# Weight sums of a two-stage mixture kernel: differences on VectorE, sums as adding transfers

## The chip, the cores and the metric

The kernel runs on one core of a Trainium2 chip. The metric is the device time of one execution in microseconds (us). In the profile PE is TensorE (PEld its weight loads), DVE is VectorE, ACT is ScalarE, POOL is GpSimd and SP is SyncE, which issues most transfers.

## The reference

Attention (a band of keys and block summaries), then a mixture in which each token goes to one expert, then a second mixture in which all 1536 tokens go through all 8 experts. The change touches the weights of the second mixture alone:

```python
def _moe2_ref(x, w_gate, w1, w2):
    N, D = x.shape                       # 1536, 512
    E = w_gate.shape[1]                  # 8
    logits = x @ w_gate
    ...                                  # 8 turns that normalise P over experts and tokens
    for e in range(E):
        h = np.maximum(x @ w1[e], 0.0)   # w1[e]: 512 x 1024
        ye = h @ w2[e]                   # w2[e]: 1024 x 512
        out += P[:, e:e + 1] * ye
```

## The kernel before

The second mixture starts at about 320 us of the span and lasts to its end. Both products of an expert are computed by a scheme of Strassen's kind: each matrix is cut into four quarters, and seven products of quarters, or of sums of quarters, replace eight. An fp32 factor is split into an fp16 part and an fp16 rest (`hi` and `lo`), and three products of these stand for one.

The program of this part is written out by hand in *ticks*. In a tick PE does one step of the first product (`first`, L1251: six matmuls into `fx` or `fa`) and, in every other tick, one step of the second product (`second`, L1337: twelve matmuls into `gx` or `ga`). One expert's first products take 84 ticks: 3 chunks of 512 tokens, 4 blocks `fc` of hidden units, 7 ticks each. Everything else is put at a tick by `at(tick, f)`, and each engine runs its instructions in the order in which the ticks issue them. In each block of seven ticks the engines do this beside PE:

- ACT copies products out of PSUM (`take`, L1258), ACT or DVE adds the others (`add`, L1261).
- For the block before, DVE forms the four sums of the hidden quarters in place in `c` (L1297 to L1300, fp32, 128x256 each), ACT casts them to fp16 (L1303, `hh`), and DVE forms the rest (L1306, `hl`). ACT reaches L1303 in its own order, and the `take`s of the next block stand behind it.
- Results of `second` go to `acc` by DVE (L1368) or by ACT into `y` (L1376), which POOL issues as an adding transfer (L1370, L1378).

The weights of the coming expert are prepared in the same ticks. A `Piece` is one of the four blocks of w1 or w2 of an expert; a raw buffer `raw` holds six quarters of 128x256 fp32, and three buffers take turns. A piece goes through: `load` (SP, ticks ahead), for most pieces `measure` (ACT, its square sum), `measured` and `rate` (a power of two as scale), `sums(0)`, `sums(1)`, `sums(2)` and `sum4` (L707 and L711: the four sums of quarters, on POOL), `raw_hi` and `raw_lo` (the three plain quarters: ACT L715 and DVE L720, 128x768), `sum_hi` and `sum_lo` (the four sums: the same lines, 128x1024). In one step three quarters are overwritten in place, so that `sum4` may run only when `raw_lo` has read the plain ones. `begin` is the tick of `raw_hi`; `raw_lo`, `sum4` follow one and two ticks later, `sum_hi` and `sum_lo` six and seven ticks later. For the last piece of w2 (`last`) these ticks hang on a step of `second`. `weigh(e)` (L1204) scales the expert's gate column `pws` at the start of its second product.

The eight pieces of expert 0 are prepared during the first mixture (`plain`), and there DVE forms the sums. In the transposition of the tokens (`tokens`, `part4`, L1077) the rests of `T3` and `T4` are formed by POOL for five of six pairs.

Of the kernel before, what the change touches and what calls it, by code (L numbers as in the profile page):

```python
# [18 lines left out]
ALU = mybir.AluOpType  # L19
# [30 lines left out]
K2 = KC // 2  # L50
# [58 lines left out]
def body(ctx: ExitStack, tc: tile.TileContext, q, k, v, wg1, w1a, w2a, wg2, w1b, w2b, cst, out):  # L109
    nc = tc.nc  # L110
# [41 lines left out]
    with ExitStack() as st:  # L152
# [29 lines left out]
        for i in range(3):  # L182
            t = a1.tile([P, NW, 2, D], F32, name=f"vt{i}")
            eng = nc.gpsimd if i else nc.vector
# [42 lines left out]
        sums = {}  # L227
# [58 lines left out]
        def queries(u):  # L286
# [26 lines left out]
            out=wg2_sb.rearrange("p (k e) -> p k e", k=KC), in_=wg2.rearrange("(k p) e -> p k e", p=P)  # L313
# [248 lines left out]
        for t in range(S // P, NTB):  # L562
# [3 lines left out]
            out=nb3,  # L566
            in0=cnt.unsqueeze(2).to_broadcast([P, E, 6]),
            in1=c_(C_BEG, 6 * E).rearrange("p (e j) -> p e j", e=E),
            op=ALU.is_gt,
# [5 lines left out]
            out=bs3,  # L575
            in0=nb.unsqueeze(1).to_broadcast([P, E, E]),
            in1=c_(C_LT, E * E).rearrange("p (e f) -> p e f", e=E),
            op=ALU.mult,
# [5 lines left out]
            out=bend, in0=nb[0:1], scalar=float(CAP), in1=base[0:1], op0=ALU.mult, op1=ALU.add  # L584
# [3 lines left out]
            out=eb3,  # L588
            in0=bend.unsqueeze(1).to_broadcast([1, NBLK, E]),
            in1=c_(C_BLK, NBLK * E)[0:1].rearrange("p (n e) -> p n e", e=E),  # L590
            op=ALU.is_le,
# [8 lines left out]
        with tc.issue_after(eblk.ins):  # L600
# [7 lines left out]
            out=at_tile,  # L608
# [54 lines left out]
    class Piece:  # L663
# [35 lines left out]
            nc.tensor.matmul(pf, ones_b, sqb[self.x][:, self.i : self.i + 1], start=True, stop=True)  # L699
            pow2(pf, wsc[self.x][:, self.i : self.i + 1], gsc[self.x][:, self.i : self.i + 1])  # L700

        def sums(self, only=None, eng=nc.gpsimd):
            o = own[id(self.raw)]; assert o is self, (self.e, self.second, self.j, o.e, o.second, o.j)
            r = [self.raw[:, i] for i in range(6)]
            todo = ((4, 3, 0, -1), (5, 4, 1, -1), (3, 3, 1, -1)) if self.second else ((5, 0, 3, -1), (4, 5, 1, -1), (3, 3, 1, 1))
            for to, x, y, sign in todo if only is None else todo[only : only + 1]:
                eng.tensor_tensor(out=r[to], in0=r[x], in1=r[y], op=ALU.add if sign > 0 else ALU.subtract)  # L707

        def sum4(self, eng=nc.gpsimd):
            o = own[id(self.raw)]; assert o is self, (self.e, self.second, self.j, o.e, o.second, o.j)  # L710
            eng.tensor_tensor(out=self.raw[:, 2], in0=self.raw[:, 2], in1=self.raw[:, 5 if self.second else 4], op=ALU.add)  # L711

        def hi(self, w, s):
            o = own[id(self.raw)]; assert o is self, (self.e, self.second, self.j, o.e, o.second, o.j)
# [135 lines left out]
    if True:  # L850
# [112 lines left out]
        def plain(i, p):  # L963
            idle = lambda: None
            raw = raws[i % 3]
            junk = raw[:, 4:6].rearrange("p a f -> p (a f)").bitcast(BF16)
            return [lambda: p.load(raw), idle, idle, lambda: p.measure(junk), p.measured, p.rate, lambda: (p.raw_hi(), p.sums(eng=nc.vector)), lambda: (p.raw_lo(), p.sum4(eng=nc.vector)),
                    idle, p.sum_hi, p.sum_lo]

        more = weave(  # L970
# [72 lines left out]
    def tokens(j):  # L1043
# [30 lines left out]
        def parts(to, x, eng):  # L1074
            hi, lo = (y[:, to[0] : to[-1] + 1, :, cols].rearrange("p a k t -> p (a k) t") for y in (sh, sl))
            nc.scalar.copy(hi, x)  # L1076
            eng.tensor_tensor(out=lo, in0=x, in1=hi, op=ALU.subtract)  # L1077
# [25 lines left out]
            parts((B22,), quarters()[3], nc.vector)  # L1103

        def part4():
            parts((T3, T4), t4[:, 2 * K2 :], nc.gpsimd if j else nc.vector)

        def part5():
            b12 = quarters()[2]
# [211 lines left out]
    def second(e, k, s, i):  # L1321
# [18 lines left out]
        if (k, s) == (CHUNKS - 1, 1) and e + 1 in last:  # L1340
            if i == 4:
                p4 = last[e + 1]
                for d, f in zip((0, 1, 2, 5, 6), (p4.raw_hi, p4.raw_lo, p4.sum4, p4.sum_hi, p4.sum_lo)):
                    at(clock[0] + 1 + d, f)
        ts = [2 * k + s + h * HTB for h in range(2)]
        lo, hi, both = slice(0, Q), slice(Q, DM), slice(0, DM)
# [93 lines left out]
    for want, p, begin, measure in sorted(jobs, key=lambda x: x[0]):  # L1440
        i = min(range(len(raws)), key=lambda i: (max(free[i], want), -free[i]))
        load = max(free[i], want)
        s = TICKS * CHUNKS * p.e
        at(load, lambda p=p, i=i: p.load(raws[i]))
        if measure:
            junk = raws[i][:, 4:6].rearrange("p a f -> p (a f)").bitcast(BF16)
            at(load + 5, lambda p=p, junk=junk: p.measure(junk))
            at(load + 7, p.measured)
            at(load + 11, p.rate)
            assert load + 11 <= s - 3, (p.e, p.second, p.j, load - s)  # L1450
            end = load + 5
        if begin is not None:
            for i_ in range(3):
                at(load + 7 + i_, lambda p=p, i_=i_: p.sums(i_))
            if p.second and p.j == F2 - 1:
                last[p.e] = p
                end = s + 41
                assert load < s + 18, (p.e, p.second, p.j, load - s)
            else:
                begin = max(begin, load + 13)  # L1460
                at(begin, p.raw_hi)
                at(begin + 1, p.raw_lo)
                at(begin + 2, p.sum4)
                end = begin + 7
                at(end - 1, p.sum_hi)
                at(end, p.sum_lo)
                assert end <= s + (39 if p.second else 7 * p.j + 1), (p.e, p.second, p.j, end - s)
                assert begin <= s + (37 if p.second else 7 * p.j - 1), (p.e, p.second, p.j, begin - s)
        free[i] = end + 1
# [53 lines left out]
```

## Time and profile before

| | us |
|---|---|
| median of 3 runs | 1281.98 |
| lowest and highest run | 1281.65, 1283.81 |
| the profiled execution: time | 1283.4 |
| the profiled execution: span, first to last instruction | 1281.5 |

| engine | busy us | share of the span |
|---|---|---|
| PE | 1194.4 | 93% |
| DVE | 1024.4 | 80% |
| ACT | 848.9 | 66% |
| POOL | 368.1 | 29% |

The profiled execution lies 1.4 us above the median, and 1.9 us of it lie outside the span. Shares of the whole span mix three parts of the program; what a change in the second mixture is worth is to be read from the stretch from 320 us on, and from who waits for whom there.

### The profile page before, as it was taken

To read this page: it belongs to the slowest core of one execution; us is meant where nothing else is said; L and a number is where in the kernel's file an instruction comes from. 1 tells how busy PE (TensorE), PEld (TensorE's weight loads), DVE (VectorE), ACT (ScalarE), POOL (GpSimd) and SP (SyncE) were. 2 spreads that over 40 slices of the span, in tenths; PEclk is the share of its full clock that TensorE was granted. 3 is DMA by queue.
4 is the path that set the end of the run, shared out by engine and by line. 5 is a ranking of instruction groups with operands and counts; after the bars stand their busy time and mean duration, and the time that the engine had idled before them with its cause. 6 is when DMAs were issued, how large, how long until landed. Compare 5 with 4: busy or idle time off the path is not lost.

```text
span 1281.5 us, 27664 instructions
## 1 busy us (share of the span) xinstructions
PE 1194.4 (93%) x10551; PEld 1050.3 (82%) x10551; DVE 1024.4 (80%) x1801; ACT 848.9 (66%) x1605; POOL 368.1 (29%) x434
## 2 busy tenths in 40 slices
PE   6898999998799899889999998999899899989998
PEld 5776878887678788778888887888788788878887
DVE  6785678874788888797988798788979888886765
ACT  5676578764777667666767776677667667766541
POOL 4351212112113443332332333242413333322000
PEclk8899999999999999999999999999999999999999
DMA  9954888755325343445543563544445435534301
GB/s 203 204 98 147 275 258 258 243 189 179 122 96 175 110 119 93 113 111 137 133 108 91 127 171 91 131 110 108 124 132 147 114 79 138 143 93 106 84 34 50
DMA packets 178461, 174.38 MB, mean 136 GB/s; under 512 B 32960, under 2 KB 150336, under 8 KB 177936
## 3 DMA queue, kind: packets, MB, share of 16 engines
q1 hardware_dynamic: 163888, 143.75, 38.7%
q0 software_dynamic: 14432, 28.78, 11.5%
q8 instruction: 85, 1.39, 0.5%
q14 instruction: 56, 0.46, 0.1%
HBM read 136.10 MB, written 15.53 MB: 118 GB/s over the span
## 4 chain that ended last, share of the span: by engine, by line
PE 55%; DVE 20%; ACT 9%; DMA 8%; issue 7%; SPq 1%; POOL 0%; DVEq 0%; ACTq 0%; POOLq 0%
PE gx L1337 13%; PE fx L1251 13%; PE fa L1251 10%; PE ga L1337 10%; DMA raw<-in_moe_w 4%; PE ph L814 3%; PE py L833 2%; DVE c L1297 2%; DVE w2l L720 2%; ACT raw L690 2%; DVE c L1298 2%; DVE c L1261 2%; DVE w1l L720 2%; DVE c L1299 1%; DVE hl L1294 1%
## 5 line engine op out<-in xcount | busy, mean ns | idle before, releaser
L1251 PEld LDWEIGHTS <-w1h 128*128 128x128 f16 x2688 | 259.5, 98 | 75.6 <-issue 42.8
L1337 PEld LDWEIGHTS <-hh 128*128 128x128 f16 x2688 | 264.0, 98 | 32.5 <-issue 1.2
L1251 PE MATMUL fx<-xh,w1h 128*128 128x256 f16 x736 | 201.1, 273 | 31.5 <-ACT c L1258 29.7
L1337 PE MATMUL gx<-w2l,hh 128*128 128x256 f16 x768 | 210.4, 274 | 3.0 <-DVE w2l L720 3.0
L1337 PE MATMUL gx<-w2h,hh 128*128 128x256 f16 x768 | 210.5, 274 | 1.0 <-DVE acc L1368 1.0
L1337 PE MATMUL gx<-w2h,hl 128*128 128x256 f16 x768 | 210.3, 274 | 0.0
L1251 PE MATMUL fx<-xl,w1h 128*128 128x256 f16 x736 | 201.3, 274 | 1.0 <-POOL xl L1077 1.0
L1251 PE MATMUL fx<-xh,w1l 128*128 128x256 f16 x736 | 201.4, 274 | 0.0
L707 POOL TENSOR_TENSOR raw<-raw 128x256 f32<-128x256 f32 x168 | 162.3, 975 | 66.0 <-ACT raw L690 41.5
L1303 ACT CAST hh<-c 128x1024 f16<-128x1024 f32 x96 | 100.2, 1043 | 116.0 <-DVE c L1300 115.9
L1258 ACT ACTIVATE c<-fx,kap 128x256 f32<-128x256 f32 x288 | 132.6, 471 | 58.3 <-PE fx L1251 57.7
L1306 DVE TENSOR_TENSOR hl<-c,hh 128x1024 f16<-128x1024 f32 x96 | 123.7, 1288 | 42.8 <-ACT hh L1303 42.7
L1337 PE MATMUL ga<-w2h,hh 128*128 128x256 f16 x576 | 157.2, 273 | 0.0
L1337 PE MATMUL ga<-w2l,hh 128*128 128x256 f16 x576 | 157.1, 273 | 0.0
L1337 PE MATMUL ga<-w2h,hl 128*128 128x256 f16 x576 | 157.0, 273 | 0.0
L1251 PE MATMUL fa<-xh,w1h 128*128 128x256 f16 x552 | 150.8, 273 | 0.9 <-ACT xh L1076 0.9
L1251 PE MATMUL fa<-xl,w1h 128*128 128x256 f16 x552 | 150.8, 273 | 0.5 <-DVE xl L1077 0.5
L1251 PE MATMUL fa<-xh,w1l 128*128 128x256 f16 x552 | 150.7, 273 | 0.0
L1337 PEld LDWEIGHTS <-hl 128*128 128x128 f16 x1344 | 132.0, 98 | 19.8 <-issue 4.1
L1251 PEld LDWEIGHTS <-w1l 128*128 128x128 f16 x1344 | 132.0, 98 | 17.9 <-issue 1.6
L1294 DVE SCALAR_TENSOR_TENSOR hl<-c,hh 128x768 f16<-128x768 f32 x96 | 94.8, 988 | 19.7 <-ACT hh L1291 19.4
L1376 ACT ACTIVATE y<-gx,pws 128x256 f32<-128x256 f32 x144 | 68.1, 473 | 62.3 <-PE gx L1337 34.4
(262 smaller groups left out, 2625.1 us busy)
## 6 DMA issues: line engine op xcount, KB each, us to landing
raw<-in_moe_w SPq DMA_DIRECT2D x64, 512.0 KB, 4.6
raw<-in_moe_w SPq DMA_DIRECT2D x228, 128.0 KB, 2.9
xh<-xohd SPq DMA_DIRECT2D x147, 128.0 KB, 3.0
xl<-xold SPq DMA_DIRECT2D x147, 128.0 KB, 3.2
acc<-y POOLq DMA_DIRECT2D x72, 256.0 KB, 4.3
raw<-in_moe_w SPq DMA_DIRECT2D x38, 256.0 KB, 3.3
vt<-in_v SPq DMA_DIRECT2D x16, 240.0 KB, 9.3
raw<-yd SPq DMA_DIRECT2D x12, 260.0 KB, 3.0
```

The costliest lines, as they stand in the source:

```text
L690: nc.scalar.activation(junk, raw, AF.Square, accum_out=ssq[self.x][:, self.i : self.i + 1])
L707: eng.tensor_tensor(out=r[to], in0=r[x], in1=r[y], op=ALU.add if sign > 0 else ALU.subtract)
L720: nc.vector.scalar_tensor_tensor(out=lo[:, w], in0=self.raw[:, s], scalar=wsc[self.x][:, self.i : self.i + 1], in1=hi[:, w], op0=ALU.mult, ...
L814: nc.tensor.matmul(ph, a, c[:, kc], start=kc == 0 and m == 0, stop=kc == KC - 1 and m == 2)
L833: nc.tensor.matmul(pys[s], a, c, start=fc == 0 and m == 0, stop=fc == FC - 1 and m == 2)
L1251: nc.tensor.matmul(p, l[:, a, kc * P : (kc + 1) * P], r[:, j, kc], start=new and kc == 0 and m == 0, stop=kc == K2 - 1 and m == 2, skip_gr ...
L1258: nc.scalar.activation(c[:, q], p, f, scale=k_)
L1294: nc.vector.scalar_tensor_tensor(out=h[1][:, :3], in0=raw, scalar=0.0, in1=h[0][:, :3], op0=ALU.max, op1=ALU.subtract)
L1303: nc.scalar.copy(h[0][:, 3:], c)
L1306: nc.vector.tensor_tensor(out=h[1][:, 3:], in0=c, in1=h[0][:, 3:], op=ALU.subtract)
L1337: nc.tensor.matmul(p, l, r, start=new and f == 0 and m == 0, stop=f == F2 - 1 and m == 2, skip_group_check=True)
L1376: nc.scalar.activation(gs[h][:, d], p, AF.Copy, scale=w)
```

## The change

For the experts 1 to 7 the sums of quarters leave POOL's arithmetic. A difference is now a `tensor_tensor` on DVE; a sum whose target already holds one of its terms is now an adding transfer that POOL issues (`add`, from SBUF to SBUF, 128x256 fp32). By the instruction lists POOL loses 168 + 56 tensor operations of 128x256; DVE gains 140 at `sums` and 7 at `sum4` (the `last` pieces); POOL issues 77 adding transfers, 28 of them at `sums(2)` of w1 pieces and 49 at `sum4`. `part4` goes wholly to DVE. Three tick rules change: `sum_hi` and `sum_lo` come eight and nine ticks after `begin` instead of six and seven; a piece that is not measured again may begin 8 ticks after its load instead of 13; for `last` pieces `sum_hi` and `sum_lo` come one tick earlier.

```diff
--- before.py
+++ after.py
@@ -699,16 +699,26 @@
             nc.tensor.matmul(pf, ones_b, sqb[self.x][:, self.i : self.i + 1], start=True, stop=True)
             pow2(pf, wsc[self.x][:, self.i : self.i + 1], gsc[self.x][:, self.i : self.i + 1])
 
-        def sums(self, only=None, eng=nc.gpsimd):
+        def add(self, to, of):
+            nc.gpsimd.dma_start(out=self.raw[:, to], in_=self.raw[:, of], accum_op=ALU.add)
+
+        def sums(self, only=None, fast=False):
             o = own[id(self.raw)]; assert o is self, (self.e, self.second, self.j, o.e, o.second, o.j)
             r = [self.raw[:, i] for i in range(6)]
             todo = ((4, 3, 0, -1), (5, 4, 1, -1), (3, 3, 1, -1)) if self.second else ((5, 0, 3, -1), (4, 5, 1, -1), (3, 3, 1, 1))
             for to, x, y, sign in todo if only is None else todo[only : only + 1]:
-                eng.tensor_tensor(out=r[to], in0=r[x], in1=r[y], op=ALU.add if sign > 0 else ALU.subtract)
-
-        def sum4(self, eng=nc.gpsimd):
+                if sign > 0 and not fast:
+                    self.add(to, y)
+                else:
+                    nc.vector.tensor_tensor(out=r[to], in0=r[x], in1=r[y], op=ALU.add if sign > 0 else ALU.subtract)
+
+        def sum4(self, fast=False):
             o = own[id(self.raw)]; assert o is self, (self.e, self.second, self.j, o.e, o.second, o.j)
-            eng.tensor_tensor(out=self.raw[:, 2], in0=self.raw[:, 2], in1=self.raw[:, 5 if self.second else 4], op=ALU.add)
+            of = 5 if self.second else 4
+            if fast:
+                nc.vector.tensor_tensor(out=self.raw[:, 2], in0=self.raw[:, 2], in1=self.raw[:, of], op=ALU.add)
+            else:
+                self.add(2, of)
 
         def hi(self, w, s):
             o = own[id(self.raw)]; assert o is self, (self.e, self.second, self.j, o.e, o.second, o.j)
@@ -964,7 +974,7 @@
             idle = lambda: None
             raw = raws[i % 3]
             junk = raw[:, 4:6].rearrange("p a f -> p (a f)").bitcast(BF16)
-            return [lambda: p.load(raw), idle, idle, lambda: p.measure(junk), p.measured, p.rate, lambda: (p.raw_hi(), p.sums(eng=nc.vector)), lambda: (p.raw_lo(), p.sum4(eng=nc.vector)),
+            return [lambda: p.load(raw), idle, idle, lambda: p.measure(junk), p.measured, p.rate, lambda: (p.raw_hi(), p.sums(fast=True)), lambda: (p.raw_lo(), p.sum4(fast=True)),
                     idle, p.sum_hi, p.sum_lo]
 
         more = weave(
@@ -1103,7 +1113,7 @@
             parts((B22,), quarters()[3], nc.vector)
 
         def part4():
-            parts((T3, T4), t4[:, 2 * K2 :], nc.gpsimd if j else nc.vector)
+            parts((T3, T4), t4[:, 2 * K2 :], nc.vector)
 
         def part5():
             b12 = quarters()[2]
@@ -1340,7 +1350,7 @@
         if (k, s) == (CHUNKS - 1, 1) and e + 1 in last:
             if i == 4:
                 p4 = last[e + 1]
-                for d, f in zip((0, 1, 2, 5, 6), (p4.raw_hi, p4.raw_lo, p4.sum4, p4.sum_hi, p4.sum_lo)):
+                for d, f in zip((0, 1, 2, 4, 5), (p4.raw_hi, p4.raw_lo, lambda: p4.sum4(True), p4.sum_hi, p4.sum_lo)):
                     at(clock[0] + 1 + d, f)
         ts = [2 * k + s + h * HTB for h in range(2)]
         lo, hi, both = slice(0, Q), slice(Q, DM), slice(0, DM)
@@ -1457,11 +1467,11 @@
                 end = s + 41
                 assert load < s + 18, (p.e, p.second, p.j, load - s)
             else:
-                begin = max(begin, load + 13)
+                begin = max(begin, load + (13 if measure else 8))
                 at(begin, p.raw_hi)
                 at(begin + 1, p.raw_lo)
                 at(begin + 2, p.sum4)
-                end = begin + 7
+                end = begin + 9
                 at(end - 1, p.sum_hi)
                 at(end, p.sum_lo)
                 assert end <= s + (39 if p.second else 7 * p.j + 1), (p.e, p.second, p.j, end - s)
```

On DVE, between expert 2 and expert 3: `w1l1` and `w1l0` are rests of weights of expert 3's w1 pieces 1 and 0, the rows of `c` alone are the hidden sums (L1297 to L1300). Before:

```order
L720 SCALAR_TENSOR_TENSOR w1l0_1677<-raw1_1711,wsc1_1699,w1h0_1676 128x1024
L1294 SCALAR_TENSOR_TENSOR hl_10066<-c_9862,hh_10065 128x768
L1261 SCALAR_TENSOR_TENSOR c_9979<-fx_9978,kap0_1700,c_9979 128x256
L1368 SCALAR_TENSOR_TENSOR acc_5495<-ga_9944,pws_5498,acc_5495 128x512
L720 SCALAR_TENSOR_TENSOR w1l1_1679<-raw2_1712,wsc1_1699,w1h1_1678 128x768
L694 CAST sqb1_1695<-ssq1_1693 128x1
L1297 SCALAR_TENSOR_TENSOR c_9862<-c_9862 128x256
L1298 TENSOR_TENSOR c_9862<-c_9862 128x256
L1299 TENSOR_TENSOR c_9862<-c_9862 128x256
L1300 TENSOR_TENSOR c_9862<-c_9862 128x256
```

And now (the same lines of the program stand ten lines lower, so L1307 is the old L1297, L1316 the old L1306 that makes the rest `hl` of the sums, L730 the old L720):

```order
L730 SCALAR_TENSOR_TENSOR w1l1_1679<-raw2_1712,wsc1_1699,w1h1_1678 128x768
L694 CAST sqb1_1695<-ssq1_1693 128x1
L713 TENSOR_TENSOR raw1_1711<-raw1_1711 128x256
L1307 SCALAR_TENSOR_TENSOR c_9861<-c_9861 128x256
L1308 TENSOR_TENSOR c_9861<-c_9861 128x256
L1309 TENSOR_TENSOR c_9861<-c_9861 128x256
L1310 TENSOR_TENSOR c_9861<-c_9861 128x256
L730 SCALAR_TENSOR_TENSOR w1l0_1677<-raw0_1710,wsc1_1699,w1h0_1676 128x1024
L713 TENSOR_TENSOR raw1_1711<-raw1_1711 128x256
L627 TENSOR_SCALAR gsc1_1697<-pz_5486 128x1
L630 TENSOR_SCALAR wsc1_1699<-gsc1_1697 128x1
L1316 TENSOR_TENSOR hl_10065<-c_9861,hh_10064 128x1024
```

One difference of the next piece (L713) stands ahead of the four hidden sums and one behind them, and the long rest of piece 0 (128x1024), which stood four rows ahead of that of `w1l1`, comes behind the four sums and ahead of `hl`.

On ACT at the same place (L1258, L1303, L1376 and L715 of before are L1268, L1313, L1386 and L725 now). Before:

```order
L715 ACTIVATE w1h0_1676<-raw1_1711,wsc1_1699 128x1024
L690 ACTIVATE raw0_1710,ssq1_1693<-raw0_1710 128x1024
L1291 ACTIVATE hh_10065<-c_9862 128x768
L715 ACTIVATE w1h1_1678<-raw2_1712,wsc1_1699 128x768
L1258 ACTIVATE c_10107<-fx_10106,kap0_1700 128x256
L1271 ACTIVATE c_9979<-c_9979 128x512
L1376 ACTIVATE y_10061<-gx_9910,pws_5498 128x256
L1258 ACTIVATE c_10107<-fa_10124,kap0_1700 128x256
L1303 CAST hh_10065<-c_9862 128x1024
```

And now:

```order
L690 ACTIVATE raw1_1711,ssq1_1693<-raw1_1711 128x1024
L1301 ACTIVATE hh_10064<-c_9861 128x768
L725 ACTIVATE w1h1_1678<-raw2_1712,wsc1_1699 128x768
L725 ACTIVATE w1h0_1676<-raw0_1710,wsc1_1699 128x1024
L1268 ACTIVATE c_10106<-fx_10105,kap0_1700 128x256
L1281 ACTIVATE c_9979<-c_9979 128x512
L1386 ACTIVATE y_10061<-gx_9910,pws_5498 128x256
L1268 ACTIVATE c_10106<-fa_10120,kap0_1700 128x256
L1313 CAST hh_10064<-c_9861 128x1024
```

The 128x1024 cast of piece 0 (`w1h0`), which stood at the head of these rows, is now between the 128x768 cast of piece 1 and the copy of `fx`.

On POOL, from the same place on, where L707 and L711 are the sums of weights and L1370 and L1378 the adding transfers of results. Before:

```order
L707 TENSOR_TENSOR raw0_1710<-raw0_1710 128x256
L711 TENSOR_TENSOR raw2_1712<-raw2_1712 128x256
L707 TENSOR_TENSOR raw0_1710<-raw0_1710 128x256
L1378 DMA acc_5495<-y_10061 128x512
L707 TENSOR_TENSOR raw0_1710<-raw0_1710 128x256
L711 TENSOR_TENSOR raw0_1710<-raw0_1710 128x256
L707 TENSOR_TENSOR raw1_1711<-raw1_1711 128x256 x3
L1370 DMA acc_5495<-y_10178 128x512
L1378 DMA acc_5495<-y_10324 128x512
```

And now (L703 is the new adding transfer, L1380 and L1388 those of results):

```order
L703 DMA raw2_1712<-raw2_1712 128x256
L1388 DMA acc_5495<-y_10061 128x512
L703 DMA raw1_1711<-raw1_1711 128x256 x2
L703 DMA raw0_1710<-raw0_1710 128x256
L1380 DMA acc_5495<-y_10178 128x512
L703 DMA raw0_1710<-raw0_1710 128x256
L1388 DMA acc_5495<-y_10324 128x512
```

Only issues of transfers are left on POOL there, each result's transfer with one or two of the weights' ahead of it.

## Rows read from the trace of the kernel before

**Rows 1.** Windows: busy us (count) by engine, PEclk, DMA share, GB/s.

```profile
330.00:480.00 150.00, 136.86 (x1318) 119.42 (x1318) 126.80 (x263) 104.73 (x197) 51.25 (x64) 0.98 0.42 129
480.00:1160.00 680.00, 648.97 (x5905) 575.38 (x5904) 580.79 (x909) 477.13 (x826) 225.49 (x262) 0.99 0.47 119
```

**Rows 2.** Waits, 480 to 1160 us: total us, times, longest us.

```profile
ACT hh L1303 <- DVE c L1300: 97.7, 53, 5.5
...
PE fx L1251 <- ACT c L1258: 28.0, 16, 2.8
...
PE gx L1337 <- DVE w2l L720: 3.0, 6, 0.6
```

**Rows 3.** Timeline 667 to 676 us: start, us; in brackets idle before.

```profile
667.21 1.01 DVE L720 SCALAR_TENSOR_TENSOR w1l<-raw,wsc,w1h 128x768 f16<-128x768 f32 x1
...
668.20 3.11 DVE L1297 SCALAR_TENSOR_TENSOR c<-c 128x256 f32<-128x256 f32 x1
...
668.42 1.04 POOL L707 TENSOR_TENSOR raw<-raw 128x256 f32<-128x256 f32 x1
...
671.35 1.34 DVE L1298 TENSOR_TENSOR c<-c 128x256 f32<-128x256 f32 x1
...
673.64 1.04 ACT L1303 CAST hh<-c 128x1024 f16<-128x1024 f32 x1 [5.30 <-DVE c L1300]
...
675.12 0.27 PE L1251 MATMUL fx<-xh,w1h 128*128 128x256 f16 x1 [2.68 <-ACT c L1258]
```

**Rows 4.** DVE groups, 480 to 1160 us: busy us, mean ns | idle before.

```profile
L1298 DVE TENSOR_TENSOR c<-c 128x256 f32<-128x256 f32 x69 | 49.4, 716 | 2.4
L1297 DVE SCALAR_TENSOR_TENSOR c<-c 128x256 f32<-128x256 f32 x69 | 44.9, 650 | 0.0
L1299 DVE TENSOR_TENSOR c<-c 128x256 f32<-128x256 f32 x69 | 44.3, 642 | 2.4
L1300 DVE TENSOR_TENSOR c<-c 128x256 f32<-128x256 f32 x69 | 38.4, 557 | 2.4
...
L1204 DVE TENSOR_SCALAR pws<-pw,winv 128x12 f32<-128x12 f32 x7 | 14.0, 2003 | 0.0
```

**Rows 5.** DVE groups, 1194 to 1250 us.

```profile
L1298 DVE TENSOR_TENSOR c<-c 128x256 f32<-128x256 f32 x6 | 2.6, 426 | 0.2
```

**Rows 6.** Timeline 490 to 493 us.

```profile
491.75 0.23 DVE L1204 TENSOR_SCALAR pws<-pw,winv 128x12 f32<-128x12 f32 x1
```

**Rows 7.** Timeline 796 to 801.5 us.

```profile
798.53 0.83 DVE L1300 TENSOR_TENSOR c<-c 128x256 f32<-128x256 f32 x1
...
799.39 1.04 ACT L1303 CAST hh<-c 128x1024 f16<-128x1024 f32 x1 [3.67 <-DVE c L1300]
...
800.87 0.27 PE L1251 MATMUL fx<-xh,w1h 128*128 128x256 f16 x1 [1.27 <-ACT c L1258]
```

**Rows 8.** POOL groups, 480 to 1160 us.

```profile
L707 POOL TENSOR_TENSOR raw<-raw 128x256 f32<-128x256 f32 x144 | 140.0, 981 | 65.6 <-ACT raw L690 41.5 <-DMA xl<-xold 20.9
```

**Rows 9.** Clock: windows inside two stretches of half clock.

```profile
560.20:563.60 3.40, 3.40 (x17) 2.34 (x17) 3.25 (x6) 2.87 (x4) 0.00 (x0) 0.50 0.30 82
676.30:679.60 3.30, 3.30 (x18) 2.36 (x16) 3.27 (x7) 2.51 (x5) 0.00 (x0) 0.50 0.28 86
```

**Rows 10.** Timeline 591 to 593 us.

```profile
591.50 0.87 POOL L1370 DMA_DIRECT2D acc<-y  x1 [9.95 <-ACT c L1258]
...
591.79 0.42 DVE L1299 TENSOR_TENSOR c<-c 128x256 f32<-128x256 f32 x1
```

**Rows 11.** DMA issues: count, KB each, median us to landing.

```profile
acc<-y POOLq DMA_DIRECT2D x72, 256.0 KB, 4.3
...
acc<-y POOLq DMA_DIRECT2D x6, 128.0 KB, 2.7
```

**Rows 12.** Timeline 656 to 666 us.

```profile
656.63 1.00 DVE L720 SCALAR_TENSOR_TENSOR w1l<-raw,wsc,w1h 128x768 f16<-128x768 f32 x1
...
665.16 0.92 ACT L715 ACTIVATE w1h<-raw,wsc 128x768 f16<-128x768 f32 x1
```

## The prediction

> **What bounds the kernel now.** I read first where PE stands idle, since every product of the second mixture passes through it. The windows [rows 1] show PE busy 648.97 us of the 680 us from 480 to 1160 us, so 31.0 us are idle there; DVE is busy 580.79 us, 85%, and POOL 225.49 us. The matmuls themselves run close to one rate (648.97 us over 5905 of them, 0.110 us each), and the change leaves their number alone. So all that can be won in this stretch is the 31.0 us and whatever the stalls drag behind them. In the two stretches [rows 1] PE is idle 31.0 and 13.1 us; the attention, the first mixture and the last expert are not touched by this change.
>
> Who ends the idle time, the table of waits says [rows 2]: PE's `fx` matmul waited 16 times, 28.0 us in all, for ACT's copy of a product out of PSUM (L1258), and six times, 3.0 us, for DVE's `w2l` (L720). Together that is the 31.0 us. ACT was late because it stood 97.7 us, 53 times, in front of its cast `hh` (L1303) waiting for DVE's fourth hidden sum (L1300); the copies are queued behind that cast. Not each wait reaches PE: 53 waits of ACT make 16 stalls of PE.
>
> The timeline of one place [rows 3] shows the cause. DVE's L1297 starts at 668.20 and takes 3.11 us, L1298 takes 1.34, and meanwhile POOL has begun its run of weight sums at 668.42. ACT's `hh` starts 5.30 us late, PE 2.68 us late. The groups of the stretch [rows 4] say how much: means of 716, 650, 642 and 557 ns for L1298, L1297, L1299 and L1300. In a stretch in which POOL does no arithmetic the same L1298 takes 426 ns [rows 5]. So DVE operations whose inputs both lie in SBUF are stretched while POOL computes. The excess over 426 ns, 69 times each: 20.0 + 15.5 + 14.9 + 9.0 = 59.4 us. L1204 (128x12) takes 2003 ns in the mean [rows 4] against 0.23 us where it stands free [rows 6]: seven times 1.77, 12.4 us. That is 71.8 us of DVE's 580.79.
>
> **What the change removes.** POOL's tensor operations go, and with them, by the above, the stretching. What that does to the stalls I work out at the two kinds of place. At the first kind [rows 3] the excess is (3.11 - 0.43) + (1.34 - 0.43) = 3.6 us of the 5.30 us that ACT waits. At the second kind [rows 7] the last three hidden sums take about 0.83 us instead of 0.43, 1.2 us of a wait of 3.67 us. PE's stalls there are 2.68 and 1.27 us, so ACT may be 2.6 or 2.4 us late before PE notices: 5.30 - 2.68 and 3.67 - 1.27. I take 2.4.
>
> **What it adds on DVE.** 126 of the 147 new operations fall in this stretch: 144 sums stood on POOL there [rows 8], three for each piece, so 48 pieces, half of w2 with three differences and half of w1 with two, which makes 120, and one `sum4` for each of six `last` pieces. Their form is that of L1298, so 426 ns each [rows 5], 53.7 us: less than the 71.8 us that go, hence DVE ends some 18 us less busy. Where they stand counts more. By the order lists one difference comes ahead of the hidden sums at the first place, and the long rest of a weight piece, which was ahead, moves behind them. ACT's wait becomes 5.30 - 3.6 + 0.43 = 2.1 us, below 2.4. At the second place both differences come behind the sums: 3.67 - 1.2 = 2.5 us, at the edge, and the long rest that was ahead of it goes behind too, which takes it under. Both margins are thin, 0.3 us and an unknown one. What is late next is `hl` (L1306) with that rest ahead of it; PE needs `hl` some ticks later in the second product. I leave 4.0 us of stalls in the sum for this, about 0.6 us for each of seven changes of expert; the bounds are 0 and 15 us.
>
> So the first term is -28.0 + 4.0 = -24.0 us. The second: the `w2l` waits come behind a stretched L1204, 2.0 us of which 1.8 go, against stalls of 0.5 us each: -3.0 us (bounds -3.0 and 0).
>
> The third is the clock. After two of the long stalls the granted clock stands at 0.50, that is 1.2 GHz instead of 2.4, for 3.4 and 3.3 us [rows 9]; about 17 matmuls pass where 0.110 us each would let 31 pass. Half of 6.7 us is lost there, and it comes back with the stalls: -3.4 us (bounds -3.4 and 0).
>
> **The transfers.** 77 new issues on POOL take the place of 224 tensor operations of 981 ns [rows 8]. An issue took 0.87 us [rows 10], and DVE's L1299 beside it took 0.42 us, so issuing does not stretch DVE as arithmetic does. No row shows an adding transfer within SBUF of a weight quarter; the nearest are the adding transfers of `y`, of the same kind: 2.7 us from issue to landing for 128 KB, which is a quarter's size, and 4.3 us for 256 KB [rows 11]. I take 2.7. What waits for them is ACT's `sum_hi`, and behind it in ACT's queue stand the copy of `fx`, the relu, a result and the next `hh`. The room: at piece 0 of w1 the plain rest ended at 657.63, and ACT now comes to the long cast behind the cast that ended at 666.08 [rows 12]. That leaves 8.4 us for a transfer of 2.7 to 4.3 us. The two more ticks of room come to 2 x 12 matmuls x 0.110 = 2.6 us. On POOL the result transfers stand behind those of the weights, which wait for DVE's `raw_lo`; before, they stood behind the same sums doing 1 us of arithmetic each. I put the term at 0, bounds 0 and the rival below. The Trainium skill speaks against this step: "SBUF — State Buffer", section "SBUF: two separate sides", says that descriptors of a transfer issued from GpSimd wait while VectorE holds the shared port pair in a two-port mode, with 620 ns growing to 3100 ns in its example. The 0.87 us beside a running DVE [rows 10] doesn't show it (L1299 is a `tensor_tensor`, for which the page's section "Who interferes with whom" counts no two-port mode); by the page, five times 0.87 us is an estimate of 4.4 us for an issue, 3.5 us more to landing, which the 8.4 us would still hold, so the sum would be the same.
>
> **From 330 to 480 us** the same forces act with less room: 13.1 us idle, DVE busy 126.80 of 150 [rows 1], the pieces of expert 1 and five `part4` steps come onto DVE. Gain and loss may cancel; term 0, bounds -5 and +5.
>
> **Sum.** -24.0 - 3.0 - 3.4 + 0 + 0 = -30.4 us. From the profiled execution's 1283.4 us that is 1253.0; the median lies 1.4 us under that execution, so 1251.6 us.
>
> **Rivals.**
>
> *DVE takes the gain back.* The differences are bunched where expert changes; if they hold `hh` as much as the stretching did, in the ratio of the two sums (53.7 to 71.8, 75%), a quarter of 34.4 us is left: 1281.98 - 8.6 = 1273 us. For it: DVE at 85%, margins of 0.3 us. Against it: the order, which puts most differences behind the hidden sums, and the rest of 1.3 us that moves behind too. Between this and my forecast lies a band around 1263 us where half is kept.
>
> *Slower: the transfers land late.* ACT stands at `sum_hi`, and PE stalls once the landing comes more than 8.4 + 2.4 = 10.8 us after `raw_lo`. With 49 `sum4` transfers the gain of 30.4 us is used up at 0.6 us each: it decides at 11.4 us, and at 12.5 us it costs 49 x 1.7 = 83 us, 1335 us in all. For it: POOL's queue goes in order and its transfers wait for DVE; the page above. Against it: 2.7 and 4.3 us [rows 11].
>
> *No change: the stretching stays*, because issuing for the transfers holds DVE as arithmetic did. Then the differences add DVE work and the time stays at 1282 or goes above it. Against it is the 0.42 us beside an issue [rows 10].
>
> **How the numbers follow.** My forecast, with its own range of 1243 to 1260 us (all bounds on the good side: -28.0 - 3.0 - 3.4 - 5 = -39.4, 1242.6 us; residual stalls of 10 us and 2 us lost before 480 us: 1259.6 us), gets 0.70. The band and the rival of DVE, 1260 to 1276 us, get 0.17, two thirds of it below 1270 us. Late transfers get 0.06, no change 0.04, and 0.03 is for a time under 1242.5 us. The range from 1242.5 to 1270 us holds 0.70 + 0.11 = 0.81. A difference under 0.2% (2.6 us) can't be told from none. Faster: 0.70 + 0.17 + 0.03 = 0.90; of the no change case 0.03 falls within 0.2%; slower 0.06 + 0.01 = 0.07.
>
> **What the profile of the changed kernel would show.** L1297 to L1300 (ten lines lower) at about 420 ns in the mean, `pws` at 0.23 us, the new differences at 426 ns; waits of `hh` for the sums all under about 2.5 us; PE's waits for ACT's copy under 5 us in all from 480 us on, and no stretch of half clock there. The new transfers land in 3 to 4 us, and ACT's `sum_hi` waits for none. I would be wrong if ACT waits at `sum_hi` for a transfer, if the hidden sums are still stretched, or if PE finds a new wait, for `hl` or for weights that now come two ticks later.

## The result and the profile after

The changed kernel takes 1248.87 us (median of 4 runs, 1246.3 to 1249.3), the kernel before 1282.89 us in the same comparison (4 runs): a ratio of 0.9729, 95% interval 0.971 to 0.9749. Forecast were 1251.6 us. The profiled execution took 1248.7 us with a span of 1246.9 us, 34.6 us less than the span of before.

In the page, the shares of the chain that ended last are for PE 75% now, 55% before; for DVE 9%, 20% before.

Times in the two traces run apart, so I compare stretches between the same two instructions: the `pws` of expert 1 and that of expert 7. First the window of before, then that of after (length, then busy us and count of PE, PEld, DVE, ACT, POOL, then PEclk, DMA share, GB/s):

```profile
491.70:1190.60 698.90, 668.31 (x6082) 592.87 (x6082) 592.29 (x927) 485.78 (x842) 224.45 (x260) 1.00 0.46 118
```

```profile
489.70:1156.50 666.80, 662.33 (x6083) 592.11 (x6081) 550.97 (x1049) 491.52 (x842) 120.76 (x138) 1.00 0.58 137
```

The stretch is 32.1 us shorter with the same matmuls. PE's idle time falls from 30.6 us (698.90 - 668.31) to 4.5 us: 26.1 us. The other 6.0 us come out of PE's busy time, and the point-by-point part says how. Of the 2.5 us left, 2.0 are won ahead of this stretch and 0.5 behind it.

The waits of after, answering to [rows 2] (480 to 1126 us, about the stretch of the program that ended at 1160 us before; total us, times, longest):

```profile
POOL raw L703 <- DVE w2l L730: 93.8, 11, 9.8
...
ACT hh L1313 <- DVE c L1310: 18.9, 20, 1.9
...
ACT y L1386 <- DMA acc<-y: 10.2, 12, 2.2
...
PE fx L1261 <- ACT c L1268: 3.3, 2, 2.2
...
PE gx L1347 <- DVE w2l L730: 1.1, 1, 1.1
...
PE fx L1261 <- DMA xl<-xold: 0.8, 1, 0.8
...
PE fx L1261 <- DMA xh<-xohd: 0.4, 1, 0.4
```

ACT stands in front of `hh` for 18.9 us where it stood 97.7, and never longer than 1.9 us; PE's 28.0 us behind ACT's copy are 3.3. POOL waits 93.8 us with its adding transfers for DVE's rest `w2l`. ACT's `sum_hi` (L725) has no wait for `raw<-raw` in this stretch; what ACT does wait for are the result transfers that POOL issues, 10.2 us for a free `y`.

The DVE groups, answering to [rows 4], 480 to 1126 us (busy us, mean ns | idle before):

```profile
L713 DVE TENSOR_TENSOR raw<-raw 128x256 f32<-128x256 f32 x117 | 48.0, 418 | 0.2
...
L1309 DVE TENSOR_TENSOR c<-c 128x256 f32<-128x256 f32 x70 | 29.8, 425 | 2.4
L1308 DVE TENSOR_TENSOR c<-c 128x256 f32<-128x256 f32 x70 | 29.7, 425 | 2.4
...
L1310 DVE TENSOR_TENSOR c<-c 128x256 f32<-128x256 f32 x69 | 29.3, 425 | 2.4
L1307 DVE SCALAR_TENSOR_TENSOR c<-c 128x256 f32<-128x256 f32 x70 | 29.3, 418 | 0.0
...
L719 DVE TENSOR_TENSOR raw<-raw 128x256 f32<-128x256 f32 x6 | 2.5, 420 | 0.0
L1214 DVE TENSOR_SCALAR pws<-pw,winv 128x12 f32<-128x12 f32 x6 | 2.0, 330 | 0.0
```

The hidden sums are back at the length of an undisturbed operation [rows 5], and the new differences (L713, L719) have it too.

The place of [rows 3], between expert 2 and 3, now stands at 658 us (timeline: start, us; idle before in brackets):

```profile
658.29 0.42 DVE L713 TENSOR_TENSOR raw<-raw 128x256 f32<-128x256 f32 x1
...
658.61 1.11 POOL L703 DMA_DIRECT2D raw<-raw  x1
658.62 0.42 DVE L1307 SCALAR_TENSOR_TENSOR c<-c 128x256 f32<-128x256 f32 x1
...
659.08 0.42 DVE L1308 TENSOR_TENSOR c<-c 128x256 f32<-128x256 f32 x1
...
659.70 1.82 POOL L703 DMA_DIRECT2D raw<-raw  x1
...
659.99 0.42 DVE L1310 TENSOR_TENSOR c<-c 128x256 f32<-128x256 f32 x1
...
660.34 1.28 DVE L730 SCALAR_TENSOR_TENSOR w1l<-raw,wsc,w1h 128x1024 f16<-128x1024 f32 x1
...
660.45 1.04 ACT L1313 CAST hh<-c 128x1024 f16<-128x1024 f32 x1 [0.98 <-DVE c L1310]
```

POOL issues beside all of them, 1.1 and 1.8 us long, and no DVE operation is longer for it. `hh` waits 0.98 us instead of 5.30, and PE does not stall here.

Of the transfers the page of the profile says (count, KB each, median us from issue to landing; [rows 11] had 4.3 us for the 256 KB of `y`, and 2.7 us for a `y` of 128 KB):

```profile
acc<-y POOLq DMA_DIRECT2D x72, 256.0 KB, 4.3
raw<-raw POOLq DMA_DIRECT2D x77, 128.0 KB, 3.5
```

### The profile page after: what moved, and what is told of

The parts are those of the page before. It is cut to its first block, busy times and chain, and to the rows that moved or that the text cites. A ratio compares the mean times of both kernels' runs of the same rounds, so it can differ in the third digit from the quotient of the medians.

```text
span 1246.9 us, 27628 instructions
## 1 busy us (share of the span) xinstructions
PE 1184.9 (95%) x10551; PEld 1047.9 (84%) x10551; DVE 982.9 (79%) x1953; ACT 853.3 (68%) x1605; POOL 231.9 (19%) x282
## 4 chain that ended last, share of the span: by engine, by line
PE 75%; DVE 9%; DMA 7%; ACT 5%; issue 3%; SPq 1%; DVEq 0%; POOL 0%; ACTq 0%; POOLq 0%
PE gx L1347 19%; PE fx L1261 18%; PE ga L1347 14%; PE fa L1261 13%; DMA raw<-in_moe_w 4%; PE py L843 3%; PE ph L824 2%; DVE wl L791 1%; PE pscore L411 1%; PE px L452 1%; ACT wh L790 1%; DMA xh<-xohd 1%; DVE c L1271 1%; DMA vt<-vm 1%; ACT raw L690 1%
## 5 line engine op out<-in xcount | busy, mean ns | idle before, releaser
L1261 PEld LDWEIGHTS <-w1h 128*128 128x128 f16 x2688 | 258.4, 98 | 46.9 <-issue 16.7
L1347 PEld LDWEIGHTS <-hh 128*128 128x128 f16 x2688 | 263.4, 98 | 32.1 <-issue 1.2
L1261 PE MATMUL fx<-xh,w1h 128*128 128x256 f16 x736 | 200.6, 273 | 7.9 <-ACT c L1268 5.0
L1261 PE MATMUL fx<-xl,w1h 128*128 128x256 f16 x736 | 200.7, 273 | 1.9 <-DVE xl L1087 1.1
L1261 PE MATMUL fx<-xh,w1l 128*128 128x256 f16 x736 | 200.8, 273 | 0.0
L1268 ACT ACTIVATE c<-fx,kap 128x256 f32<-128x256 f32 x288 | 134.3, 472 | 78.3 <-PE fx L1261 77.4
L1261 PE MATMUL fa<-xh,w1h 128*128 128x256 f16 x552 | 150.4, 272 | 0.9 <-ACT xh L1086 0.9
L1261 PE MATMUL fa<-xl,w1h 128*128 128x256 f16 x552 | 150.4, 273 | 0.5 <-DVE xl L1087 0.5
L1261 PE MATMUL fa<-xh,w1l 128*128 128x256 f16 x552 | 150.4, 273 | 0.0
L1261 PEld LDWEIGHTS <-w1l 128*128 128x128 f16 x1344 | 131.4, 98 | 18.7 <-issue 3.3
L1316 DVE TENSOR_TENSOR hl<-c,hh 128x1024 f16<-128x1024 f32 x96 | 117.3, 1222 | 27.7 <-ACT hh L1313 26.9
L1386 ACT ACTIVATE y<-gx,pws 128x256 f32<-128x256 f32 x144 | 68.0, 472 | 83.9 <-PE gx L1347 62.6
L1313 ACT CAST hh<-c 128x1024 f16<-128x1024 f32 x96 | 99.8, 1039 | 34.6 <-DVE c L1310 34.2
L703 POOL DMA_DIRECT2D raw<-raw x77 | 79.0, 1054 | 210.7 <-DVE w2l L730 95.3
L1271 DVE SCALAR_TENSOR_TENSOR c<-fa,kap,c 128x512 f32<-128x512 f32 x96 | 71.8, 747 | 46.7 <-PE fa L1261 39.0
```

The lines of the kernel that those rows point to most:

```text
L703: nc.gpsimd.dma_start(out=self.raw[:, to], in_=self.raw[:, of], accum_op=ALU.add)
L1261: nc.tensor.matmul(p, l[:, a, kc * P : (kc + 1) * P], r[:, j, kc], start=new and kc == 0 and m == 0, stop=kc == K2 - 1 and m == 2, skip_gr ...
L1268: nc.scalar.activation(c[:, q], p, f, scale=k_)
L1271: nc.vector.scalar_tensor_tensor(out=c[:, q], in0=x, scalar=k_, in1=c[:, q], op0=ALU.mult, op1=ALU.add)
L1313: nc.scalar.copy(h[0][:, 3:], c)
L1316: nc.vector.tensor_tensor(out=h[1][:, 3:], in0=c, in1=h[0][:, 3:], op=ALU.subtract)
```

## The experiments

**The theory:** POOL's arithmetic, because it reads SBUF, stretches DVE operations with two inputs in SBUF; its end is the gain, whoever does the sums instead. **The rivals:** the three tick rules bring the gain by reordering DVE and ACT; or any work on POOL beside DVE does the harm, reading or not; or it is the adding transfers that bring it, by keeping work off DVE. The first four kernels ran beside a kernel before of 1286.67 us (13 runs), the last four beside one of 1284.97 us (9 runs). Since the kernel before differs between these comparisons, I compare kernels by their ratios. Waits and groups of all of them are those of 480 to 1126 us; a slower kernel gets through less of the program there (5578 matmuls in experiment 2, 5882 in the changed kernel). In this window the kernel before has 87.8 us of waits of ACT's `hh` and 23.9 us of PE behind ACT's copy.

**1. The tick rules alone**, put into the kernel before:

```diff
-                for d, f in zip((0, 1, 2, 5, 6), (p4.raw_hi, ...
+                for d, f in zip((0, 1, 2, 4, 5), (p4.raw_hi, ...
...
-                begin = max(begin, load + 13)
+                begin = max(begin, load + (13 if measure else 8))
...
-                end = begin + 7
+                end = begin + 9
```

> The kernel before with the three tick rules of the change alone; all sums stay POOL arithmetic. Theory (POOL's arithmetic stretches DVE's operations, and the end of that is the gain): the hidden sums are still stretched, means of 550 to 720 ns, and the time stays within 1% of 1282.9 us, at best some 10 us lower because the long rest of a weight piece now comes behind the hidden sums. Rival (the gain is that move behind the hidden sums): 1250 to 1262 us.

Measured: 1280.09 us, ratio 0.9948 (0.9931 to 0.9965). The groups and waits of this kernel:

```profile
L1298 DVE TENSOR_TENSOR c<-c 128x256 f32<-128x256 f32 x67 | 55.1, 823 | 2.3
...
L1299 DVE TENSOR_TENSOR c<-c 128x256 f32<-128x256 f32 x67 | 45.3, 676 | 2.3
```

```profile
ACT hh L1303 <- DVE c L1300: 74.9, 38, 4.4
...
PE fx L1251 <- ACT c L1258: 23.5, 26, 1.8
```

The stretching is there as before, if anything more of it (L1298's 823 ns lie above the 720 that I expected), and PE still loses 23.5 us behind ACT. The order alone gives half a per cent of the 2.7%.

**2. POOL reads again.** Everything of the change stays; at each step that had POOL arithmetic before, 224 in all, POOL adds a tile to itself that nobody uses:

```diff
+    pad = wq.tile([P, Q], F32, name="pad")
+    def burn():
+        nc.gpsimd.tensor_tensor(out=pad, in0=pad, in1=pad, op=ALU.add)
...
-                at(load + 7 + i_, lambda p=p, i_=i_: p.sums(i_))
+                at(load + 7 + i_, lambda p=p, i_=i_: (p.sums(i_), burn()))
```

> The changed kernel, with one POOL addition of 128x256 fp32 on a tile of its own at each tick at which a sum stood on POOL before (224 in all). It waits for nothing and nothing waits for it, so it is additional work and changes no result. Theory of the stretching: the means of DVE's four hidden sums go from 420 ns back to 550 to 720 ns, and since DVE now has the differences as well, the time is 1275 to 1310 us. Rival (the gain came with the tick rules, or since DVE does the differences faster than POOL did): no change, 1246 to 1253 us. A third theory, that the gain came because POOL's queue was empty and the results' transfers left sooner, also gives about 1280 us here; the run beside it, with writes alone, tells it from the first.

Measured: 1296.98 us, ratio 1.0074 (1.0054 to 1.0095), by the ratios some 44 us above the changed kernel:

```profile
L665 POOL TENSOR_TENSOR pad<-pad 128x256 f32<-128x256 f32 x179 | 190.3, 1063 | 6.3
...
L718 DVE TENSOR_TENSOR raw<-raw 128x256 f32<-128x256 f32 x112 | 63.5, 575 | 0.2
...
L1276 DVE SCALAR_TENSOR_TENSOR c<-fa,kap,c 128x512 f32<-128x512 f32 x66 | 49.0, 743 | 7.8 <-PE pz L704 5.3 <-PE fa L1266 2.5
...
L1314 DVE TENSOR_TENSOR c<-c 128x256 f32<-128x256 f32 x66 | 43.9, 664 | 2.3
```

```profile
ACT hh L1318 <- DVE c L1315: 96.6, 45, 3.8
...
PE fx L1266 <- ACT c L1273: 25.3, 34, 1.9
```

Additions that no one waits for undo the whole gain, and the differences, now on DVE, are stretched as well. Not stretched is `c<-fa,kap,c` (L1276), which reads one of its two large inputs from PSUM: 743 ns here, 749 in the changed kernel. The single operations say the same. In the kernel before, from 480 to 1160 us, the 30 of L1298 that overlap a sum on POOL take 1094 ns in the mean and the 39 others 425, while `c<-fa,kap,c` (L1261) takes 741 ns in the 19 that overlap one and 748 in the 51 others.

**3. POOL writes only.** The same kernel, with three memsets of the same tile in place of each addition:

```diff
-        nc.gpsimd.tensor_tensor(out=pad, in0=pad, in1=pad, op=ALU.add)
+        [nc.gpsimd.memset(pad, 0.0) for _ in range(3)]
```

> As the run with POOL additions, but each addition is replaced by three POOL fills of the same tile, which read nothing from SBUF; by the fills of 128x768 and 128x1536 shape that the first part of the kernel has (732 and 1372 ns) three of them are estimated at 0.9 us, as long as an addition. If it is POOL's queue or its being busy that costs: 1275 us or more, as with additions. If it is its reading that collides with DVE operations whose two inputs lie in SBUF: hidden sums at 420 to 430 ns and 1246 to 1256 us. The Trainium skill, "SBUF — State Buffer", section "Who interferes with whom", says that a VectorE instruction with two SBUF inputs contends with a GpSimd instruction that reads SBUF and not with one that only writes it.

Measured: 1247.66 us, ratio 0.969 (0.9665 to 0.9715), no more than the changed kernel:

```profile
L665 POOL MEMSET pad<- 128x256 f32 x576 | 220.0, 382 | 26.9
...
L1313 DVE TENSOR_TENSOR c<-c 128x256 f32<-128x256 f32 x70 | 29.8, 425 | 2.4
```

POOL is at work longer than in experiment 2 (220.0 us against 190.3), at the same places, and DVE's sums take 425 ns. So it is not POOL's being busy but what its operation does: the additions read SBUF, the memsets only write it. The Trainium skill says this in "SBUF — State Buffer", section "Who interferes with whom": a DVE instruction with two SBUF inputs contends with a GpSimd instruction that reads SBUF, not with one that only writes it. The 664 and 425 ns agree. The memsets are also shorter than the additions, 382 ns against 1063, and no run has long operations on POOL beside these sums that only write.

**4. All sums on DVE**, no adding transfers:

```diff
-                if sign > 0 and not fast:
-                    self.add(to, y)
-                else:
+                if True:
                     nc.vector.tensor_tensor(out=r[to], in0=r[x], in1=r[y], ...
...
-            if fast:
+            if True:
                 nc.vector.tensor_tensor(out=self.raw[:, 2], in0=self.raw[:, 2], ...
```

> The changed kernel with no adding transfers for weights: all 224 sums on DVE, 77 more operations at 0.42 us, 32 us in all, some 28 of them between 480 and 1160 us where DVE was busy 562 of 680 us. Theory: DVE has the room, most of these operations stand behind the hidden sums or in slack ticks: 1246 to 1256 us, stalls of PE for ACT's copies under 8 us in that stretch. Rival (the adding transfers are what makes the change work, because DVE is the next bound): stalls at each change of expert as before, 1262 us or more.

Measured: 1252.07 us, ratio 0.9734 (0.9712 to 0.9756), not to be told from the changed kernel. DVE is busy 559.39 us of 646 against 538.97, `hh` waits 29.6 us against 18.9 but never more than 2.3 us, and PE waits 2.8 us for ACT's copy. The transfers aren't what brings the gain: DVE has room for all 224 sums. Between the `pws` of expert 1 and of expert 7 (495.5 to 1158.7 us) DVE is busy 570.0 us with all of these sums on it, where it was busy 592.3 us before with none.

**5. The change without the tick rules:** the edit of experiment 1 taken back in the changed kernel.

> The changed kernel with the three tick rules of before: sum_hi and sum_lo six and seven ticks after begin, 13 ticks from load to begin, the old ticks for last pieces. It tries the room of the adding transfers, which shrinks by two ticks (2.6 us) to about 5.8 us where the prediction had 8.4, and puts the long rest of a piece ahead of the hidden sums again (1.3 us on DVE). Theory: the transfers (median 3.5 us to landing in the changed kernel) still come in time for most pieces, the hidden sums come up to 1.3 us later and bring back stalls of 1 us or less at the changes of expert: 1250 to 1260 us. If the tick rules are needed because transfers would be late: ACT waits for them at its casts, 1262 us or more. If the rules are worth nothing beside the differences on DVE: 1246 to 1250 us.

Measured: 1259.99 us, ratio 0.98 (0.978 to 0.9821), above the changed kernel's interval. ACT's and PE's waits:

```profile
ACT hh L1313 <- DVE c L1310: 52.5, 38, 2.6
...
ACT w1h L725 <- DMA raw<-raw: 9.7, 12, 2.0
...
ACT w2h L725 <- DMA raw<-raw: 2.5, 6, 0.4
```

```profile
PE fx L1261 <- ACT c L1268: 11.5, 18, 1.9
```

The sums take 425 ns here too, so the loss isn't stretching. ACT waits 12.2 us for transfers that land too late for the old `sum_hi`, 20.6 us for a free `y` where it is 10.2 us in the changed kernel, and 52.5 us for hidden sums that stand behind DVE's long rests, where it is 18.9. With the new ticks all three are smaller or gone; which of them costs how much no run separates. Arithmetic off POOL gives 2.0% by itself, and the tick rules 0.7% on top of it (0.98 to 0.9729).

**6. Half the arithmetic back on POOL:** the 77 adding transfers become POOL additions, the differences stay on DVE.

```diff
-            nc.gpsimd.dma_start(out=self.raw[:, to], in_=self.raw[:, of], accum_op=ALU.add)
+            nc.gpsimd.tensor_tensor(out=self.raw[:, to], in0=self.raw[:, to], in1=self.raw[:, of], op=ALU.add)
```

> The changed kernel, with the 77 adding transfers as POOL additions in place again; the differences stay on DVE. A dose between before (224 POOL additions) and now (none). Theory: stretching goes with the number of POOL operations that DVE meets: about a third of the excess of before, some 25 us on DVE between 480 and 1160 us, means of the hidden sums 460 to 530 ns; the time between the two kernels, 1254 to 1270 us. If the adding transfers themselves cost something that POOL additions don't: 1249 us or less. If what counts is only that the three-sum bursts of POOL are gone: 1246 to 1252 us.

Measured: 1254.37 us, ratio 0.9763 (0.9738 to 0.9788); its interval overlaps that of the changed kernel.

```profile
L703 POOL TENSOR_TENSOR raw<-raw 128x256 f32<-128x256 f32 x66 | 63.8, 970 | 205.0 <-DVE w2l L730 93.5 <-issue 85.6 <-DVE raw L713 14.3
...
L1308 DVE TENSOR_TENSOR c<-c 128x256 f32<-128x256 f32 x69 | 45.4, 657 | 2.4
```

```profile
ACT hh L1313 <- DVE c L1310: 60.0, 33, 3.2
...
PE fx L1261 <- ACT c L1268: 6.0, 9, 1.1
```

Two of the four sums are stretched nearly as much as before (657 and 620 ns; 709 and 645 in this window of the kernel before), ACT waits 60.0 us, and yet PE loses 6.0 us. ACT's longest wait is 3.2 us: 26 of the 33 stay under 2.4 us, and the four of 2.52 us cost PE nothing. So the price of stretching isn't proportional to it; it depends on whether the chain of sums, cast and copy uses up what PE has in hand at that place.

**7 and 8. The rest before 480 us.** PE idles 13.1 us from 330 to 480 us before [rows 1] and after. Experiment 7 moves the only POOL arithmetic left in the normalisation of the gate weights to DVE; experiment 8 adds earlier ticks for `rate` of the first pieces.

```diff
-            nc.gpsimd.tensor_tensor(out=pw, in0=pw, in1=r.unsqueeze(2).to_broadcast(sh), op=ALU.mult)
+            nc.vector.tensor_tensor(out=pw, in0=pw, in1=r.unsqueeze(2).to_broadcast(sh), op=ALU.mult)
...
-            for p, i, load, square, rate in ((p1[3], 1, -23, -18, -13), (p2[3], 0, -23, -16, -10), ...
+            for p, i, load, square, rate in ((p1[3], 1, -23, -18, -14), (p2[3], 0, -23, -16, -12), ...
```

> The changed kernel with the 16 POOL multiplications of the gate's normalisation (pw, 128x96) on DVE too, so that POOL computes nothing in the second mixture. Two of these turns hold up PE for 0.7 and 1.0 us in the changed kernel (its matmul pz waits for DVE's c, which waits for POOL). Theory: the hand-over to POOL and the stretching of what is left go: 1 to 3 us less than the changed kernel, 1245 to 1248 us; a ratio to before of 0.970 to 0.973. Rival (DVE is full between 400 and 480 us): no change or 1 to 2 us more.

> As the run without POOL arithmetic, and the scales (rate) of four pieces of expert 1 are taken at other ticks: 14, 12, 9 and 7 ticks ahead of the expert instead of 13, 10, 7 and 4, so that no two matmuls of rate stand one tick apart; in both kernels the second of such a pair held PE up for 2.40 us, because the small PSUM tile was not read yet by DVE (L627). Theory: that stall goes, 2 to 3 us less than the run without it, 1242 to 1246 us. Rival (DVE's lag moves to the next matmul that needs it): no difference between the two runs.

Measured: 1252.8 us, ratio 0.9735 (0.9707 to 0.9762), and 1251.73 us, 0.9739 (0.9722 to 0.9756): no difference from the changed kernel, where I had expected 1245 to 1248 and 1242 to 1246 us; in both the rival came. In 7 PE's longest wait there is as it was, 2.6 us for DVE's `gsc` (2.4 in the changed kernel). In 8 that one is gone, and PE waits at the next small matmuls instead: 3.1 us for `c` of the normalisation (1.7 in the changed kernel), 1.7 us for `gsc`, 1.4 us for another `c`. The lag of DVE moves to the small matmuls that come next. No version tried beats the changed kernel beyond its interval.

## Why the prediction was right, point by point

**The cause** held: experiment 2 against 3 shows that POOL's additions stretch DVE's operations and POOL's fills don't, and operations that read an input from PSUM were left alone. The rival that the stretching stays beside transfers falls with the 425 ns, and the rival that DVE takes the gain back with experiment 4.

**The stall term**, -28.0 + 4.0 in the sum, is -28.0 + 3.3 in the waits. That the 4.0 comes so near is luck: it was put there for `hl`, for which PE never waits, and both stalls of the 3.3 us come before 515 us and have other causes (below). The room of 2.4 us before PE notices holds for the two kinds of place it was read from, where it is 2.6 and 2.4 us: in experiment 6 waits of 2.52 us cost nothing and two of 2.92 us cost 0.29 each. It isn't one number for the whole stretch: in the kernel before a wait of 2.25 us that ended at 523.37 us made a stall of 0.76, a room of 1.5 us, and experiment 5 has six stalls of 0.2 to 0.6 us behind waits of 2.09. Now no wait of `hh` is above 1.9 us. At the place of [rows 3] I had 2.1 us for the wait and measured 0.98. The largest stall left, 2.2 us, is that of a result's buffer:

```profile
513.87 0.47 ACT L1386 ACTIVATE y<-gx,pws 128x256 f32<-128x256 f32 x1 [2.11 <-DMA acc<-y]
...
514.76 0.37 PE L1261 MATMUL fx<-xh,w1h 128*128 128x256 f16 x1 [2.20 <-ACT c L1268]
```

ACT reuses a `y` whose adding transfer, issued at 508.12, landed only then; the `take` that PE needs stands behind it. Such waits of ACT came to 8.6 us before (480 to 1160 us), with a stall of 1.99 us at this place (515.94), and come to 10.2 us now; experiment 4 has 9.7 without any weight transfer, so they aren't the weight transfers'. The other stall, 1.1 us at 494.01, stands behind three operations of ACT on weights and has no counterpart before. A third buffer for `y` was not tried.

**The `w2l` term**, -3.0, is -3.0 + 1.1: one of six stalls stays. Two new stalls of 0.8 and 0.4 us wait for loads of `xl` and `xh`.

**The clock term** was -3.4. Between the two `pws` the granted clock fell to 0.50 twice before [rows 9] and once now, as the 2.20 us stall ends (window 514.60 to 517.90):

```profile
514.60:517.90 3.30, 3.14 (x15) 2.16 (x15) 1.40 (x3) 3.30 (x6) 0.00 (x0) 0.50 0.46 140
```

15 matmuls pass there instead of 30. So half of the term came. "No stretch of half clock from 480 us on" was wrong.

**A term that I left out** makes up for it, which is luck too. Of the 6.0 us by which PE's busy time fell, one stretch of half clock fewer gives 1.7. Most of the rest lies in how idle time counts a stall. A matmul's row is 0.27 us long, but in a run of matmuls the next starts 0.11 us behind it; idle time begins only where the row ends, so of a stall's step from start to start 0.16 us more than the idle time are lost. Steps over 0.26 us fell from 26 to 5; 21 x 0.16 = 3.4 us, and 0.9 us stay unassigned. So a stall costs its idle time and 0.16 us more, and the sum priced each of the 22 stalls of [rows 2] too low by that. That is worked out from the starts in the trace, not tested by a run of its own.

**DVE's account** was off on the right side: in the windows above its busy time fell by 41.3 us, where some 18 were foreseen. By the groups between the two `pws`, hidden sums and `pws` lost 71.3 us (71.8 foreseen), the differences cost 50.9 us (53.7), and the rests `hl` and of the weights, which also read two tiles in SBUF, lost some 10 us that I had not counted. That makes some 30 us; the other 11 come of counting, for the rows of neighbouring DVE operations overlap, by 40 us in all in the first window and 52 in the second, and busy time counts an overlap once. `pws` takes 330 ns in the mean and not the 230 foreseen.

**The transfers** were put at 0, and with the new ticks that held: no wait of ACT. The landing takes 3.5 us, not 2.7, and an issue 1.07 us in the mean, not 0.87. My room of 8.4 us was one place's; experiment 5 shows that with two ticks fewer (2.6 us) ACT waits up to 2.0 us, so by an estimate from these two the tightest piece now has some 0.6 us to spare. The Trainium skill ("SBUF — State Buffer", "SBUF: two separate sides") tells of a transfer issued from GpSimd that takes 620 ns alone and 3100 ns beside a VectorE copy in a two-port mode. The 66 issues here take 1.07 us in the mean and 1.82 at most; no run shows whether an operation of DVE beside them was in such a mode, so this neither bears the page out nor speaks against it.

**330 to 480 us**, term 0 with 5 us to either side: 2.0 us were won up to the `pws` of expert 1. PE's idle time from 330 to 480 us is as before (13.1 us), but the granted clock is 1.00 in the mean, where [rows 1] had 0.98: before had two stretches of half clock there, of 3.4 us each, and after has none. Experiments 3, 4, 6 and 7 show two again, at nearly the same waits, so by these runs the gain before 480 us isn't the change's for certain.

The sum of -30.4 us stood at -34.7 by the profiled executions. The stall term, which carries most of it, came by the mechanism foreseen; the terms that were too good (`w2l` by 1.1 us, the clock by 1.7, the loads by 1.2) were more than made up by what had no term, the 3.4 us beside idle time and the 2.0 us before 480 us.

## What to carry to other kernels

When an engine's operations of one shape have very different lengths in different stretches, compare them with what another engine does meanwhile before counting them as work: here GpSimd arithmetic that reads SBUF cost VectorE more time (592.3 us busy) than doing the same sums itself (570.0 us). What such stretching costs depends on the slack of the chain behind it, 1.5 to 2.6 us by place here: a wait within the slack cost almost nothing, one beyond it a stall and sometimes the clock. Adding transfers take sums off the engines for free only where their reader comes late enough at the tightest place, not at the typical one; here the kernel without them was as fast.

## What the hardware showed that was not expected

A small DVE operation stood still behind a whole run of POOL's, not behind one. In the kernel of experiment 1:

```profile
617.12 0.87 POOL L1378 DMA_DIRECT2D acc<-y  x1 [1.31 <-ACT y L1376]
...
617.50 2.64 DVE L1204 TENSOR_SCALAR pws<-pw,winv 128x12 f32<-128x12 f32 x1
...
617.69 1.73 POOL L711 TENSOR_TENSOR raw<-raw 128x256 f32<-128x256 f32 x2
...
619.06 1.04 POOL L707 TENSOR_TENSOR raw<-raw 128x256 f32<-128x256 f32 x1
```

`pws` started 0.19 us before POOL's first sum and ended with the third, 2.64 us later instead of 0.23. Beside one addition it took 0.65 us (experiment 2, median), beside an issue on POOL that had begun before it 0.35 us (changed kernel, median), and beside a memset 0.23 us (experiment 3, five times). Like the sums it is held by POOL's additions and not by its memsets; but beside `pw` it reads only the scalar column `winv`, and it started ahead of the operations that held it. What it waits for there stays open.

A long stall was not always followed by half clock. Of the six stalls of 2.7 to 2.8 us from 480 us on in the kernel before, the first two (558.83 and 675.12 us) were followed by it and the four others (790.84, 906.64, 1022.81 and 1138.40 us) were not. A stall of 2.4 us at about 430 us was followed by it in the kernel before and in experiment 3, and not in the changed kernel. What tells them apart stays open.
